# The attention stage's instructions put in an order computed by a list scheduler, with three PSUM tiles shared by mixing, scores and v's products

## The chip, the cores and the metric

The kernel runs on one core of a Trainium2 chip. The metric is the device time of one execution in microseconds, as the median of several runs; smaller is better. All five engines of the core work side by side, each through its own list of instructions in the order in which the program issues them: TensorE (PE; PEld are its weight loads), VectorE (DVE), ScalarE (ACT), GpSimd (POOL) and SyncE (SP). An instruction that waits holds up what stands behind it on its engine. POOL, SP and ACT also issue the transfers (DMA).

## The reference

Talking-heads attention, followed by a feed-forward part with a learned slope for negative values:

```python
scores = scale * np.matmul(q, k.transpose(0, 1, 3, 2))          # q, k, v: (4, 12, 448, 64)
scores = np.einsum('bhij,hg->bgij', scores, w_pre)              # heads are mixed
scores = scores - np.max(scores, axis=-1, keepdims=True)
attn = np.exp(scores)
attn = attn / (np.sum(attn, axis=-1, keepdims=True) + 1e-09)
attn = np.einsum('bhij,hg->bgij', attn, w_post)                 # and mixed again
x = np.matmul(attn, v)                                          # -> (1792, 768)
h = x @ w_in                                                    # w_in: (768, 2048), float64
g = np.maximum(h, 0.0) + alpha * np.minimum(h, 0.0)
out = g @ w_out                                                 # (1792, 768), w_out float64
```

## The kernel before

**Tiling.** Each of the 4 batches is cut into four chunks of query rows: 120, 120, 120 and 90 (`CHUNKS`, L27; two rows of the last chunk are computed twice). There are NC = 16 chunks. A chunk is cut again into groups of 10 rows with all 12 heads, 120 rows in all; there are NG = 180 groups, and two groups make one step, NB = 90 steps. A step is called m, and it has these parts:

- *Scores, Q* (`qk`, L143): six tiles for each chunk, 96 in all; a tile holds two heads, four matmuls of 64 x 64, or 64 x 56 in a chunk of 120 and 64 x 26 in a chunk of 90 for the second part of the rows. `qk_out` (L158) copies the tile from PSUM to an SBUF tile st, one of three (`NXS`).
- *Relay, L* (`relay`, L167): a transfer from SBUF to SBUF that gathers one group's rows and heads (210 KB) into one of eight buffers sr.
- *Mixing, M* (`mix`, L172): two groups times the mask matrix `wk`, into a PSUM tile m.
- *Maximum, R* (`rmax`, L181, DVE), *exponentials, E* (`exp`, L186, ACT, two of them), *normalising, N* (`norm`, L193, DVE, three small ones).
- *Products with w_post, P* (`post`, L204): 56 small matmuls into the PSUM tile pa, of which there is one; `post_out` (L218, called A below) copies pa in two parts to the chunk's tile at.
- *v's products, V* (`pv`, L227): two for each chunk, 48 matmuls of 128 x 64 each; `pv_out` (L239) makes an upper half (ACT, XH) and a lower half (DVE, XL) in the tile xe and leaves two stores to the scratch x2 in DRAM for the next step.

**PSUM.** It has eight banks. Mixing has two tiles of two banks (`ps_m`), scores and v's products share one tile of two banks (`ps_s`), pa has the last two (L102 to L104).

**Order.** The order is written by hand in `step(m)` (L371): the loads of this step, mixing of m + 1, the stores left over, relays up to three steps ahead, `norm(m - 1)`, `rmax(m + 1)`, `exp(m)`, one scores tile, `post(m - 2)` and its copies, then the rest of the scores and v's products. A table `jobs` (L283 to L304) says in which step the scores, the v products and the loads of q, k and v come; scores tiles come 0.92 steps apart (`WPACE`). Relays go out by SP and POOL in turn; q, k, v and raw weights are loaded by POOL, x2 and wsc are stored by SP. VectorE also turns the first three blocks of the two float64 weights into float32 (`convert`, L269, 42 operations spread over the steps), which go to the scratch wsc and are read back and split before the feed-forward part (`load_pre`, `split_w`).

**Feed-forward.** 64 units (`units`, L413) of 18 matmuls `l1`, four operations `act` and 18 matmuls `l2`. Units 0 and 1 of `l1` are issued inside the last attention steps (L553 to L558).

Of the kernel before, what the change touches and what calls it, by code (L numbers as in the profile page):

```python
# [14 lines left out]
ALU = mybir.AluOpType  # L15
# [26 lines left out]
WPACE = 0.92  # L42


def round_f64(nc, raw, e, t):
# [15 lines left out]
    yield lambda: v.tensor_tensor(tf, tf, e.bitcast(F32), ALU.mult)  # L61


@with_exitstack
def talking_heads_prelu(ctx: ExitStack, tc: tile.TileContext, q, k, v, w_pre, w_post, mask, w_in, w_out, alpha, out):
# [23 lines left out]
    p1, p1r, p1m = ExitStack(), ExitStack(), ExitStack()  # L89
# [22 lines left out]
    pa = ps_a.tile([128, 2, 512], F32, tag="a", name="pa")  # L112
# [30 lines left out]
    def qk(ci, p, ps_pool=None):  # L143
        b, c = chunk_list[ci]
        cn = CHUNKS[c][1]
        ps = (ps_pool or ps_s).tile([128, 2, 512], F32, tag="m" if ps_pool else "s", name=f"s{ci}_{p}")
# [11 lines left out]
    def qk_out(ci, p, copy=nc.scalar.copy):  # L158
        if p == 0:
            s_t[ci] = s_tile(ci % NXS, f"st{ci}")  # L160
# [6 lines left out]
    def relay(n, dma):  # L167
        ci, r = groups[n]
        sr_t[n] = sr_b[n % NSR]
        dma.dma_start(out=sr_t[n][SR0:SR0 + GP], in_=s_t[ci][r:CHUNKS[chunk_list[ci][1]][1]:CHUNKS[chunk_list[ci][1]][1] // GI])  # L170

    def mix(m):  # L172

        ps = ps_m.tile([128, 2, 512], F32, tag="m", name=f"m{m}")
# [43 lines left out]
    def post_out(m):  # L218
        for g in range(2):
            n = 2 * m + g  # L220
            ci, r = groups[n]
            if n == first[ci]:
                a_t[ci] = a_tile(f"at{ci}")[:, :NS * H * CW].rearrange("p (s h i) -> p s h i", s=NS, h=H)
            dst = a_t[ci].rearrange("p s h i -> p (s h) i")[:, :, GI * r:GI * r + GI]
            nc.vector.tensor_copy(dst, pa[:, g, :NS * GP].rearrange("p (s i) -> p s i", i=GI))  # L225

    def pv(ci, hx, ps_pool=None):  # L227
        b, c = chunk_list[ci]
        cn = CHUNKS[c][1]
        ps = (ps_pool or ps_s).tile([128, 2, 512], F32, tag="m" if ps_pool else "s", name=f"x{ci}_{hx}")  # L230
# [8 lines left out]
    def pv_out(ci, hx):  # L239
        b, c = chunk_list[ci]  # L240
        c0, cn = CHUNKS[c]
        xe = xep.tile([128, 2, 3, CW], F32R, tag="xe", name=f"xe{ci}_{hx}")
        ps = u_t.pop(("pv", ci, hx))
        hi, lo = (xe[:, i, :, :cn].rearrange("p c (k g) -> p c g k", k=GI) for i in range(2))
        src = ps[:, 0, :3 * CW].rearrange("p (c i) -> p c i", c=3)[:, :, :cn].rearrange("p c (g k) -> p c g k", k=GI)
        nc.scalar.copy(hi, src)  # L246
        nc.vector.tensor_tensor(lo, src, hi, ALU.subtract)  # L247

        def store():
            for i in range(2):  # L250
                nc.sync.dma_start(
                    out=x2[i, 3 * hx:3 * hx + 3, :, b * S + c0:b * S + c0 + cn].rearrange("c p i -> p c i"),
                    in_=xe[:, i, :, :cn].bitcast(F32))

        later.append(store)

    later = []
# [11 lines left out]
    def convert():  # L269
        todo = [(f, x) for f in range(NPRE) for x in range(2)]  # L270
        raw_c = [fetch_w(*todo[0])]
        yield
        for i, (f, x) in enumerate(todo):
            if i + 1 < len(todo):
                raw_c.append(fetch_w(*todo[i + 1]))
            t, ops = round_w(f, x, raw_c.pop(0))
            for op in ops:
                op()
                yield
            later.append(lambda f=f, x=x, t=t: nc.sync.dma_start(  # L280
                out=wsc[f, :, x * DM:(x + 1) * DM], in_=t.bitcast(F32)))

    jobs = {}  # L283

    def at(m, f, *args):
        jobs.setdefault(m, []).append((f, args))

    LEAD = 4
    uses = [(ci, p) for ci in range(1, NC) for p in range(NP)][LEAD:]
    for i, (ci, p) in enumerate(uses):  # L290
        at(int(i * WPACE), "qk", ci, p)
        b, c = chunk_list[ci]
        if c == len(CHUNKS) - 1 and b + 1 < B and p in (1, 3):
            at(int(i * WPACE) + 1, "load", load_k, b + 1, (p + 1) // 2)
    for ci, (b, c) in enumerate(chunk_list):
        if ci >= 2:
            at(max(first[ci - 2] // 2 - 1, 0), "load", load_q, ci)
        if c == 0:
            if b:
                at(first[ci] // 2 - 15, "load", load_k, b, 0)  # L300
            at(first[ci] // 2 + LAG + 3 if b else 1, "load", load_v, b)
        lb = (first[ci + 1] - 1) // 2
        at(lb + LAG + 1, "pv", ci, 0)
        at(lb + LAG + (2 if ci + 1 < NC else 1), "pv", ci, 1)  # L304
    conv_steps = NPRE * 2 * 7 + 1

    with tc.manual_schedule():
# [10 lines left out]
        def warm_up(n, name):  # L318
            ps = ps_m.tile([128, 2, 512], F32, tag="m", name=name)
# [21 lines left out]
        conv = convert()  # L341
        next(conv)
# [10 lines left out]
        relayed = 0  # L353

        def relays(upto, dmas):
            nonlocal relayed
            while relayed < min(upto, NG):
                relay(relayed, dmas[relayed % len(dmas)])
                relayed += 1

        for i in range(NP + LEAD):
            ci, p = divmod(i, NP)
            qk(ci, p, None if i % 3 == 2 else ps_m)
            qk_out(ci, p, nc.vector.tensor_copy if i % 2 else nc.scalar.copy)
            if i == NP - 1:
                relays(2 * (RAHEAD + 1), (nc.sync, nc.scalar, nc.gpsimd))
        done = 0
        live = lambda m: 0 <= m < NB
        EV = {"qk": (qk, qk_out), "pv": (pv, pv_out)}

        def step(m):  # L371
            nonlocal done
            todo = jobs.get(m, [])
            for f, args in todo:
                if f == "load":
                    args[0](*args[1:])
            uses = sorted([(f, args) for f, args in todo if f != "load"], key=lambda x: x[0] == "pv")
            early = 0 if not uses or uses[0][0] == "pv" else 1
            if live(m + 1):
                mix(m + 1)  # L380
            now, later[:] = list(later), []
            for f in now:
                f()
            if m >= 0:
                relays(2 * (m + 2 + RAHEAD) if m > 2 else first[1], (nc.sync, nc.gpsimd))
            if live(m - 1):
                norm(m - 1)
            if live(m + 1):
                rmax(m + 1)
            if live(m):  # L390
                exp(m, 0)
                exp(m, 1)
            for f, args in uses[:early]:
                EV[f][0](*args)
                EV[f][1](*args)
            if live(m - LAG):
                post(m - LAG)
                post_out(m - LAG)
            for f, args in uses[early:]:
                EV[f][0](*args)  # L400
                EV[f][1](*args)
            want = (m - 4) * conv_steps // (NB - 24)
            while done < want and done < conv_steps:
                next(conv, None)
                done += 1

# [10 lines left out]

        def load_x(bl, i):
# [5 lines left out]

        x_log, x_in = [], {}
# [17 lines left out]
        def split_w(f, x, src):  # L443
            t = (wi_t, wo_t)[x][f]
            nc.scalar.copy(t[:, 0], src)  # L445
            nc.vector.tensor_tensor(t[:, 1], src, t[:, 0], ALU.subtract)
# [27 lines left out]
        def l1(u):  # L474
            gi, bl, f = units[u]
            w, x = wi_t[f], x_t[bl].bitcast(F32R)
            ps = P2["h"].tile([128, 512], F32, tag="h", name=f"h{u}")
# [7 lines left out]

        def act(u):
            f = units[u][2]
            h = h_t.pop(u)[:, :S]
            t = P2["gp"].tile([128, S], F32, tag="t", name=f"t{u}")
            g = g_t[u] = P2["gp"].tile([128, 2, S], F32R, tag="g", name=f"g{u}")  # L490
            nc.scalar.activation(out=t, in_=h, func=AF.Relu, scale=-1.0)  # L491
            nc.vector.scalar_tensor_tensor(out=t, in0=t, scalar=oma[:, f:f + 1], in1=h, op0=ALU.mult, op1=ALU.add)  # L492
            nc.scalar.copy(g[:, 0], t)  # L493
            yield
            nc.vector.tensor_tensor(g[:, 1], t, g[:, 0], ALU.subtract)
            yield
# [150 lines left out]
```

## Time and profile before

| | us |
|---|---|
| runs shown | 996.95, 1007.74, 999.22 |
| median | 999.22 |
| the profiled execution's own time | 1001.84 |
| its span, first to last instruction | 1000.1 |

The profile is of one execution. Busy times over the whole span: PE 907.2 us (91%), its weight loads 669.0, DVE 596.1, ACT 319.9, POOL 110.6; the mean granted clock of TensorE is 0.957 of full speed, where 0.5 is its lower level (1.2 GHz) and 1.0 the upper (2.4 GHz). A PE that reads as busy need not be at its peak: matmuls are pipelined and their ends are modelled, so the time from the start of one group to the start of the next is the safer price. "Idle before, released by" names what ended an engine's wait.

### The profile page before, as it was taken

Reading aid. Unit: us, or ns where it says so; the run is one execution under the profiler, and the core shown is the slowest. Engines: PE = TensorE matmul, PEld = TensorE weight load, DVE = VectorE, ACT = ScalarE, POOL = GpSimd, SP = SyncE. Lnnn points to the kernel's source line nnn. Section 1 sums busy time; section 2 is a strip of 40 time slices with the busy share of each in tenths; the row PEclk is TensorE's granted clock in tenths of the full one; section 3 lists DMA queues with packets and bytes.
Section 4 is the critical chain, followed back from the end, with each engine's and each line's share of the span. In section 5 each row is a group of like instructions: output and inputs, shape, how many; then the busy total and the mean of one; then the engine's idle time right before and its main releaser. Section 6 shows DMA issues by size and latency. Waiting matters only on the chain.

```text
span 1000.1 us, 23702 instructions
## 1 busy us (share of the span) xinstructions
PE 907.2 (91%) x10380; PEld 669.0 (67%) x10380; DVE 596.1 (60%) x1085; ACT 319.9 (32%) x656; POOL 110.6 (11%) x193
## 2 busy tenths in 40 slices
PE   6899887998879988799589999999999999979998
PEld 2344553445534455245379999999999999869997
DVE  3556875468743787346565665766766765683222
ACT  2534553345532555233332222212112221221111
POOL 3312212111122120201000000000000000000000
PEclk9799998899978999798899999999999999989999
DMA  6764647446373464524966113201410330024111
GB/s 157 220 161 136 192 139 201 121 131 206 124 211 90 124 186 149 147 67 132 322 167 256 40 64 133 73 32 64 173 63 33 118 119 32 32 64 166 56 50 61
DMA packets 71022, 125.34 MB, mean 125 GB/s; under 512 B 32584, under 2 KB 59336, under 8 KB 70920
## 3 DMA queue, kind: packets, MB, share of 16 engines
q0 software_dynamic: 15264, 59.00, 19.6%
q1 hardware_dynamic: 54866, 63.33, 19.5%
q10 hardware_dynamic: 790, 1.52, 0.6%
q8 instruction: 81, 1.33, 0.6%
q14 instruction: 21, 0.17, 0.1%
HBM read 66.16 MB, written 18.92 MB: 85 GB/s over the span
## 4 chain that ended last, share of the span: by engine, by line
PE 74%; DVE 12%; DMA 7%; ACT 5%; issue 1%; POOL 1%; SPq 0%; DVEq 0%; ACTq 0%; POOLq 0%
PE h L481 23%; PE acc L508 22%; PE s L151 13%; PE x L235 8%; PE pa L212 5%; DMA sr<-st 3%; DMA q<-in_q_dram 3%; DVE at L225 3%; PE m L178 2%; ACT xe L246 2%; DVE xe L247 2%; DVE nm L183 2%; ACT st L163 2%; DVE ao L520 1%; DVE r L200 1%
## 5 line engine op out<-in xcount | busy, mean ns | idle before, releaser
L481 PE MATMUL h<-x,w 128*128 128x448 f32 x1152 | 251.2, 371 | 7.3 <-ACT w L445 6.9
L508 PE MATMUL acc<-g,w 128*128 128x448 f32 x1152 | 245.5, 366 | 2.1 <-DVE xe L247 1.5
L481 PEld LDWEIGHTS h<-x,w 128*128 128x128 f32 x1152 | 217.5, 189 | 30.2 <-ACT w L445 7.4
L508 PEld LDWEIGHTS acc<-g,w 128*128 128x128 f32 x1152 | 216.1, 188 | 21.5 <-DVE xe L247 1.6
L151 PE MATMUL s<-k,q 64*64 64x448 f32 (+2 forms) x768 | 174.6, 586 | 48.1 <-DMA q<-in_q_dram 18.2
L225 DVE COPY at<-pa 128x480 f32<-128x480 f32 x180 | 109.5, 649 | 101.8 <-PE pa L212 101.8
L212 PEld LDWEIGHTS pa<-r,e 64*64 64x64 f32 x5040 | 101.2, 142 | 74.0 <-DVE at L225 37.1
L151 PEld LDWEIGHTS s<-k,q 64*64 64x64 f32 (+2 forms) x768 | 40.1, 133 | 165.1 <-issue 102.7
L492 DVE SCALAR_TENSOR_TENSOR t<-t,oma,h 128x448 f32<-128x448 f32 x64 | 43.5, 679 | 154.8 <-ACT t L491 154.8
L163 ACT COPY st<-s 120x896 f32<-120x896 f32 (+1 forms) x91 | 82.2, 905 | 146.4 <-PE s L151 139.3
L190 ACT ACTIVATE e<-m,nm 128x448 f32<-128x448 f32 x180 | 112.2, 631 | 49.0 <-DVE nm L183 28.5
L212 PE MATMUL pa<-r,e 64*64 64x60 f32 x5040 | 109.4, 231 | 12.3 <-DVE at L225 11.0
L491 ACT ACTIVATE t<-h 128x448 f32<-128x448 f32 x64 | 34.8, 544 | 264.6 <-PE h L481 264.6
L178 PE MATMUL m<-sr,wk 64*64 64x448 f32 x720 | 98.5, 591 | 12.2 <-DMA sr<-st 12.0
L183 DVE TENSOR_REDUCE nm<-m 128x2 f32<-128x896 f32 x90 | 97.5, 1084 | 18.1 <-PE m L178 18.1
L235 PE MATMUL x<-at,v 128*64 128x120 f32 (+1 forms) x1536 | 81.9, 262 | 5.7 <-issue 2.1
L170 POOL DMA_DIRECT2D sr<-st x88 | 54.0, 614 | 276.4 <-PE m L178 200.8
L235 PEld LDWEIGHTS x<-at,v 128*64 128x64 f32 x1536 | 74.6, 137 | 9.7 <-ACT st L163 3.3
L247 DVE TENSOR_TENSOR xe<-x,xe 128x360 fp32r<-128x360 f32 (+1 forms) x32 | 24.0, 750 | 62.5 <-ACT xe L246 62.5
L520 DVE TENSOR_TENSOR ao<-ao,acc 128x448 f32<-128x448 f32 x96 | 52.6, 612 | 1.7 <-PE acc L508 1.7
L493 ACT CAST g<-t 128x448 fp32r<-128x448 f32 x64 | 36.3, 567 | 54.0 <-DVE t L492 54.0
L246 ACT CAST xe<-x 128x360 fp32r<-128x360 f32 (+1 forms) x32 | 24.2, 756 | 89.3 <-PE x L235 89.3
(47 smaller groups left out, 467.6 us busy)
## 6 DMA issues: line engine op xcount, KB each, us to landing
x<-x SPq DMA_DIRECT2D x16, 1344.0 KB
sr<-st SPq DMA_DIRECT2D x89, 210.0 KB
sr<-st POOLq DMA_DIRECT2D x88, 210.0 KB, 3.8
cr<-in_w_in_dram POOLq DMA_DIRECT2D x16, 768.0 KB, 4.7
cr<-in_w_out_dram POOLq DMA_DIRECT2D x16, 768.0 KB, 4.6
x<-xe SPq DMA_DIRECT2D x48, 180.0 KB
out_dram<-ao SPq DMA_DIRECT2D x24, 224.0 KB
v<-in_v_dram POOLq DMA_DIRECT2D x4, 1152.0 KB, 8.6
```

The lines of the kernel that those rows point to most:

```text
L151: nc.tensor.matmul(ps[i0:i1, hf, :S], q_t[ci][r, p * cn + i0:p * cn + i1], k_t[b, p // 2][r, p % 2, :], start=True, stop=True)
L163: copy(dst[:cn, p], u_t.pop(("qk", ci, p))[:cn, :, :S])
L170: dma.dma_start(out=sr_t[n][SR0:SR0 + GP], in_=s_t[ci][r:CHUNKS[chunk_list[ci][1]][1]:CHUNKS[chunk_list[ci][1]][1] // GI])
L178: nc.tensor.matmul(ps[hf:hf + 64, u, :S], wk[r, :], g[r, :], start=True, stop=True)
L183: nc.vector.tensor_reduce(out=nm, in_=m_t[m][:, :, :S], axis=AX.X, op=ALU.max, negate=True)
L190: nc.scalar.activation(out=e_t[m][:, u], in_=m_t[m][:, u, :S], func=AF.Exp, bias=nm_t[m][:, u:u + 1], scale=1.0, accum_out=se_t[m][:, u:u ...
L212: nc.tensor.matmul(dst[:, :, HI * u:HI * u + HI], e[h, u, 64 * jb:64 * jb + 64], r[h, u].rearrange("p (h i) -> p h i", h=H), start=True, s ...
L225: nc.vector.tensor_copy(dst, pa[:, g, :NS * GP].rearrange("p (s i) -> p s i", i=GI))
L235: nc.tensor.matmul(ps[64 * t:64 * t + 64, 0, cl * CW:cl * CW + cn], v_t[b][:, s, h * D:(h + 1) * D], a_t[ci][:, s, h, :cn], start=(s == 0) ...
L481: nc.tensor.matmul(ps[:, :S], w[:, tw, cc * 128:(cc + 1) * 128], x[:, tx, cc, :], start=(i == 0), stop=(i == 3 * NCC - 1))
L508: nc.tensor.matmul(accs[c][:, :S], w[:, tw, c * 128:(c + 1) * 128], g[:, tg], start=(f == fs[0] and i == 0), stop=(f == fs[-1] and i == 2))
L520: nc.vector.tensor_tensor(acc_sb[c, bl], acc_sb[c, bl], accs[c][:, :S], ALU.add)
```

## The change

`plan` is new. It lists every operation of the attention stage with the engines that may do it, a duration from `COST`, a priority counted in steps, the operations that it needs, and the buffers that it takes and gives back. A loop then picks, again and again, the operation with the smallest start time + 0.3 x priority, and the list sorted by start time is the order in which the program issues. Mixing, scores, v's products and the first two units of `l1` each take one of three PSUM tiles of two banks; pa stays alone. The copies S, A and XH go to ACT or DVE, as the planner finds. The waits between engines are made from the data, as before; the plan sets the order alone. `step`, `jobs`, `convert` and `later` go. The transfers are planned as one lane (dma), and each operation is issued by the same engine as before; relays alternate, the first six over SP, ACT and POOL. The feed-forward part's loop stays, but for units 0 and 1, whose `act` is planned too, and the PSUM pool of `h`, which opens later. The diff, cut:

```diff
-WPACE = 0.92
+COST = {"Q": 0.82, "M": 0.82, "P": 1.0, "V": 2.15, "U": 3.7, "mode": 0.15, "R": 1.09, "E": 1.37, "N": 0.68}
+HOP, DRAIN = 0.07, 0.2
+LOOK = 0.3
+def plan(groups, first, chunk_list):
+    for ci, (b, c) in enumerate(chunk_list):
+        op(("LQ", ci), dma(1.0) if ci >= 2 else dma(0.0, 0.0), first[max(ci - 1, 0)] / 2 - RAHEAD - 5, acq=(("q", ci),))
+        for p in range(NP):
+            n = ci * NP + p
+            prio = (n - NP) * 0.92 - 1
+            op(("Q", ci, p), pe("Q"), prio, [("LQ", ci), ("LK", b, p // 2)], (("slot", (ci, p)),) + ((("st", ci),) if p == 0 else ()),
+               ((("q", ci),) if p == NP - 1 else ()) + ((("k", b, p // 2),) if c == len(CHUNKS) - 1 and p % 2 else ()),
+               at=5.5 + 1.1 * p if ci == 0 else 10.0)
+            op(("S", ci, p), [act(0.92), dve(1.09)], prio, [("Q", ci, p)], rel=(("slot", (ci, p)),))
+    for b in range(B):
+        op(("LV", b), dma(3.0), f4 / 2 + (4 if b else 0), acq=(("v", b),), at=18.0)
+    for n, (ci, r) in enumerate(groups):
+        op(("L", n), dma(0.8, 4.0), n / 2 - 1 - RAHEAD, [("S", ci, p) for p in range(NP)], (("sr", n),),
+           (("st", ci),) if n + 1 == first[ci + 1] else ())
+    for m in range(NB):
+        op(("M", m), pe("M"), m - 1, [("L", 2 * m), ("L", 2 * m + 1)], (("slot", m),), (("sr", 2 * m), ("sr", 2 * m + 1)), at=12.0)
+        op(("R", m), dve(COST["R"]), m - 1, [("M", m)])
+        op(("E", m), act(COST["E"]), m, [("R", m)], (("e", m),), (("slot", m),))
+        op(("N", m), dve(COST["N"]), m + 1, [("E", m)], (("r", m),))
+        op(("P", m), pe("P"), m + 2, [("N", m)], (("pa", m),), (("e", m), ("r", m)))
+        for g in range(2):
+            op(("A", m, g), [act(0.52), dve(0.63)], m + 1.7, [("P", m)],
...
+            op(("V", ci, hx), pe("V", "v"), pr, mine + [("LV", b)], (("slot", (ci, hx, "v")),),
+            op(("XH", ci, hx), [act(0.8), dve(0.78)], pr, [("V", ci, hx)], (("xe", (ci, hx)),))
+            op(("XL", ci, hx), dve(0.78), pr, [("XH", ci, hx)], rel=(("slot", (ci, hx, "v")),))
+            op(("W", ci, hx), dma(1.0), pr + 1, [("XL", ci, hx)], rel=(("xe", (ci, hx)),))
...
+    cap = {"slot": 3, "st": NXS, "sr": 2 * (RAHEAD + 1), "e": LAG + 1, "r": LAG + 1, "pa": 1, "at": 2, "q": 3, "k": 4, "v": 1,
+           "xe": 2, "cr": 2, "ct": 2}
+    while ready:
+        best = None
+        for n in ready:
+            engs, prio, preds, acq, rel, at = ops[n]
+            if any(not free[kind] for kind, *_ in acq):
+                continue
+            t0 = max([at] + [end[p] for p in preds] + [min(free[kind])[0] for kind, *_ in acq])
+            for e, d, l, md in engs:
+                d += COST["mode"] if e == "PE" and md != mode else 0.0
+                t = max(t0, idle[e])
+                if best is None or (t + LOOK * prio, t) < best[0]:
+                    best = (t + LOOK * prio, t), n, e, d, l, md
...
+    return sorted(out)
@@
-    ps_m = pool("ps_m", 2, p1m, space=PSUM, side="right")
-    ps_s = pool("ps_s", 1, p1, space=PSUM)
-    ps_a = pool("ps_a", 1, p1, space=PSUM)
+    ps = pool("ps", 1, p1, space=PSUM)
+    pa = ps.tile([128, 2, 512], F32, tag="a", name="pa")
+    def slot_tile(i, name):
+        return ps.tile([128, 2, 512], F32, tag=f"b{i}", name=name)
@@
+    def relay_q(n, sr):
+        turns[0] += 1
+        dmas = (nc.sync, nc.scalar, nc.gpsimd) if n < 2 * RAHEAD else (nc.sync, nc.gpsimd)
+        relay(n, dmas[turns[0] % len(dmas)], sr)
@@
+        for _, _, n, e, got in plan(groups, first, chunk_list):
+            emit(n, e, got)
         p1.close()
         open_pool("ao", 1)
+        open_pool("h", 2, space=PSUM)
         open_pool("acc", 1, space=PSUM)
+        conv2 = convert2()
         next(conv2)
...
-            todo = [act(u)] if u < nu else []
+            todo = [act(u)] if 1 < u < nu else []
```

## Rows read from the trace of the kernel before

**Rows 1.** Stages: span, then busy of PE, PEld, DVE, ACT, POOL; clock, DMA share, GB/s.
```profile
25.70:520.50 494.80, 422.96 (x8020) 234.95 (x8020) 304.69 (x624) 218.46 (x487) 88.21 (x149) 0.92 0.54 161
...
164.00:186.00 22.00, 17.36 (x150) 5.47 (x150) 8.31 (x19) 5.17 (x13) 3.99 (x7) 0.77 0.77 209
...
284.00:312.00 28.00, 22.19 (x152) 6.65 (x152) 8.36 (x19) 5.19 (x13) 2.93 (x5) 0.63 0.51 141
...
406.00:422.00 16.00, 10.94 (x75) 3.42 (x76) 3.04 (x7) 2.24 (x5) 0.19 (x1) 0.57 0.53 155
422.00:484.00 62.00, 53.77 (x1054) 29.61 (x1052) 37.76 (x82) 24.21 (x61) 6.11 (x11) 0.94 0.42 135
...
520.50:1000.10 479.60, 468.59 (x2268) 427.04 (x2268) 281.24 (x442) 95.71 (x163) 12.91 (x24) 0.99 0.25 87
```

**Rows 2.** Order of time, PE, a step of wide scores: start, us, instruction.
```profile
237.67 0.98 PE L151 MATMUL s<-k,q 64*56 64x448 f32 x8
...
238.66 1.09 PE L212 MATMUL pa<-r,e 64*64 64x60 f32 x54
...
240.34 0.98 PE L151 MATMUL s<-k,q 64*56 64x448 f32 x8
```

**Rows 3.** Order of time, PE, a step with v's products.
```profile
230.85 2.68 PE L235 MATMUL x<-at,v 128*64 128x120 f32 x48
...
233.46 0.98 PE L178 MATMUL m<-sr,wk 64*64 64x448 f32 x8
...
235.24 0.98 PE L151 MATMUL s<-k,q 64*64 64x448 f32 x8 [0.80 <-DVE xe L247]
...
236.04 1.04 PE L212 MATMUL pa<-r,e 64*64 64x60 f32 x54
```

**Rows 4.** Order of time, PE and its weight loads, chunks of 90 rows.
```profile
53.69 3.52 PE L151 MATMUL s<-k,q 64*64 64x448 f32 x8
...
54.52 0.12 PEld L151 LDWEIGHTS s<-k,q 64*26 64x26 f32 x2 [0.71 <-issue]
...
57.14 1.09 PE L212 MATMUL pa<-r,e 64*64 64x60 f32 x54
...
513.48 2.08 PE L235 MATMUL x<-at,v 128*64 128x90 f32 x48
```

**Rows 5.** Waits of PE, 25.7 to 520.5: us in all, times, longest.
```profile
PE s L151 <- DMA q<-in_q_dram: 18.2, 3, 6.7
PE s L151 <- DVE xe L247: 18.2, 25, 0.8
PE m L178 <- DMA sr<-st: 12.0, 4, 7.6
PE pa L212 <- DVE at L225: 11.0, 17, 1.5
```

**Rows 6.** Order of time, POOL and PE, around the late load of q.
```profile
156.82 0.73 POOL L137 MEMSET v<- 64x768 f32 x1 [8.58 <-PE x L235]
...
158.84 1.06 POOL L131 DMA_DIRECT2D q<-in_q_dram  x2
...
168.64 6.64 PE L151 MATMUL s<-k,q 64*64 64x448 f32 x8 [5.04 <-DMA q<-in_q_dram]
```

**Rows 7.** Groups by shape, DVE and ACT, 25.7 to 520.5: count, busy, mean ns, idle.
```profile
L225 DVE COPY at<-pa 128x480 f32<-128x480 f32 x180 | 109.5, 649 | 101.8 <-PE pa L212 101.8
L183 DVE TENSOR_REDUCE nm<-m 128x2 f32<-128x896 f32 x90 | 97.5, 1084 | 18.1 <-PE m L178 18.1
...
L163 DVE COPY st<-s 120x896 f32<-120x896 f32 x1 | 1.1, 1091 | 4.4 <-PE s L151 4.4
...
L190 ACT ACTIVATE e<-m,nm 128x448 f32<-128x448 f32 x180 | 112.2, 631 | 49.0 <-DVE nm L183 28.5 <-PE pa L212 19.5 <-PE m L178 0.8
L163 ACT COPY st<-s 120x896 f32<-120x896 f32 x62 | 56.2, 906 | 27.2 <-PE s L151 25.8 <-DMA sr<-st 1.1
```

**Rows 8.** Transfers issued 156 to 176: count, KB each, median us to landing.
```profile
sr<-st POOLq DMA_DIRECT2D x4, 210.0 KB, 10.1
```

More of the change, by code (lines that the diff above doesn't have):

```diff
@@ L216, in a_tile, with post_out, pv @@
         return ap_.tile([128, 2 * 4 * DM], F32, tag="a", name=name)
[L218 to L227, printed above, removed]
+    def post_out(m, g, eng):
+        n = 2 * m + g
+        ci, r = groups[n]
+        if n == first[ci]:
+            a_t[ci] = a_tile(f"at{ci}")[:, :NS * H * CW].rearrange("p (s h i) -> p s h i", s=NS, h=H)
+        dst = a_t[ci].rearrange("p s h i -> p (s h) i")[:, :, GI * r:GI * r + GI]
+        copy_on[eng](dst, pa[:, g, :NS * GP].rearrange("p (s i) -> p s i", i=GI))
+    def pv(ci, hx, slot):
         b, c = chunk_list[ci]
         cn = CHUNKS[c][1]
-        ps = (ps_pool or ps_s).tile([128, 2, 512], F32, tag="m" if ps_pool else "s", name=f"x{ci}_{hx}")
+        ps = slot_tile(slot, f"x{ci}_{hx}")
         for cl in range(3):
@@ L237, in pv, with pv_out, store_x @@
         u_t["pv", ci, hx] = ps
-    def pv_out(ci, hx):
+    xe_t = {}
+    def pv_out(ci, hx, part, eng):
+        cn = CHUNKS[chunk_list[ci][1]][1]
+        if part == 0:
+            xe_t[ci, hx] = xep.tile([128, 2, 3, CW], F32R, tag="xe", name=f"xe{ci}_{hx}")
+        xe, ps = xe_t[ci, hx], u_t["pv", ci, hx]
+        hi, lo = (xe[:, i, :, :cn].rearrange("p c (k g) -> p c g k", k=GI) for i in range(2))
+        src = ps[:, 0, :3 * CW].rearrange("p (c i) -> p c i", c=3)[:, :, :cn].rearrange("p c (g k) -> p c g k", k=GI)
+        if part == 0:
+            copy_on[eng](hi, src)
+        else:
+            nc.vector.tensor_tensor(lo, src, hi, ALU.subtract)
+    def store_x(ci, hx):
         b, c = chunk_list[ci]
         c0, cn = CHUNKS[c]
[L242 to L257, printed above, removed]
+        for i in range(2):
+            nc.sync.dma_start(
+                out=x2[i, 3 * hx:3 * hx + 3, :, b * S + c0:b * S + c0 + cn].rearrange("c p i -> p c i"),
+                in_=xe_t[ci, hx][:, i, :, :cn].bitcast(F32))
     def fetch_w(f, x, dma=nc.gpsimd):
@@ L267, in round_w, with fetch, conv_op, store_w @@
         return t, round_f64(nc, raw, e, t)
[L269 to L305, printed above, removed]
+    half = lambda i: divmod(i, 2)
+    conv = {}
+    def fetch(i):
+        conv[i] = [fetch_w(*half(i))]
+    def conv_op(i, j):
+        if j == 0:
+            t, ops = round_w(*half(i), conv[i][0])
+            conv[i] = [t, list(ops)]
+        conv[i][1][j]()
+    def store_w(i):
+        f, x = half(i)
+        nc.sync.dma_start(out=wsc[f, :, x * DM:(x + 1) * DM], in_=conv[i][0].bitcast(F32))
     with tc.manual_schedule():
@@ L318, in warm_up @@
         def warm_up(n, name):
-            ps = ps_m.tile([128, 2, 512], F32, tag="m", name=name)
+            ps = slot_tile(2, name)
             for _ in range(n):
@@ L352, in talking_heads_prelu @@
         )
[L353 to L405, printed above, removed]
         P2 = {}
@@ L472, in convert2, with l1 @@
                 yield NFC
-        def l1(u):
+        def l1(u, slot=None):
             gi, bl, f = units[u]
             w, x = wi_t[f], x_t[bl].bitcast(F32R)
-            ps = P2["h"].tile([128, 512], F32, tag="h", name=f"h{u}")
+            ps = P2["h"].tile([128, 512], F32, tag="h", name=f"h{u}") if slot is None else slot_tile(slot, f"h{u}")[:, 0]
             i = 0
@@ L484, in l1, with act_op @@
             h_t[u] = ps
-        def act(u):
[L487 to L495, printed above, removed]
+        def act_op(u, j):
+            f = units[u][2]
+            h = h_t[u][:, :S]
+            if j == 0:
+                g_t[u] = (P2["gp"].tile([128, S], F32, tag="t", name=f"t{u}"),
+                          P2["gp"].tile([128, 2, S], F32R, tag="g", name=f"g{u}"))
+            t, g = g_t[u]
+            if j == 0:
+                nc.scalar.activation(out=t, in_=h, func=AF.Relu, scale=-1.0)
+            elif j == 1:
+                nc.vector.scalar_tensor_tensor(out=t, in0=t, scalar=oma[:, f:f + 1], in1=h, op0=ALU.mult, op1=ALU.add)
+            elif j == 2:
+                nc.scalar.copy(g[:, 0], t)
+            else:
+                nc.vector.tensor_tensor(g[:, 1], t, g[:, 0], ALU.subtract)
+        def act(u):
+            for j in range(4):
+                if j == 3:
+                    yield
+                act_op(u, j)
             yield
@@ L526, in talking_heads_prelu @@
         l2_done = 0
-        last = max(jobs)
-        end1 = max(NB + LAG, last + 1)
-        split_at = None
-        for m in range(-1, end1 + 1):
-            step(m)
-            if m == first[NC - 1] // 2 - RAHEAD + 1:
-                load_x(0, (NC - 3) % NXS)
-            if relayed == NG and split_at is None:
-                p1r.close()
-                open_pool("gp", 2, side="right")
-                open_pool("wA", 1, side="right")
-                for f in range(2):
-                    load_pre(f)
-                load_x(1, (NC - 2) % NXS)
-                conv2 = convert2()
-                split_at = m + 4
-            elif split_at is not None and 0 <= m - split_at < NPRE:
-                f = m - split_at
-                w_tile(f)
-                for x in range(2):
-                    split_w(f, x, wr[f][:, x * DM:(x + 1) * DM])
-                if f + 2 < NPRE:
-                    load_pre(f + 2)
-            if m == NB - 1:
-                p1m.close()
-                open_pool("h", 2, space=PSUM, side="right")
-            if m == NB:
-                l1(0)
-            if m == NB + 1:
-                for _ in act(0):
-                    pass
-                l1(1)
@@ L559, in talking_heads_prelu, with split_pre, turn @@
-        for f in later:
-            f()
+        def split_pre(f, x, part):
+            if x == 0 and part == 0:
+                w_tile(f)
+            split_w(f, x, wr[f][:, x * DM:(x + 1) * DM], part)
+        def turn():
+            p1r.close()
+            open_pool("gp", 2, side="right")
+            open_pool("wA", 1, side="right")
+        turns = [0]
+        def relay_q(n, sr):
+            turns[0] += 1
+            dmas = (nc.sync, nc.scalar, nc.gpsimd) if n < 2 * RAHEAD else (nc.sync, nc.gpsimd)
+            relay(n, dmas[turns[0] % len(dmas)], sr)
```

142 lines of the change are left out of this document (124 added, 18 removed).

## The prediction

> **What bounds the kernel now.** I read the busy table by stage first [rows 1], because the change touches one stage only. Attention fills the span up to 520.5 us, where the feed-forward part starts its steady run; from there TensorE is busy 468.59 of 479.60 us at a granted clock of 0.99. No edit reaches into that run, so I carry its 479.6 us over unchanged. From the first mixing product at 25.7 us to 520.5, 494.8 us, the mean clock is 0.92; VectorE is busy 304.69 us and ScalarE 218.46 us. The two together are 523 us, 262 each if shared evenly: neither need be the bound. PE reads 422.96 us there, but busy PE is modelled and holds waits, so I price its work from the time between starts.
>
> The order of time gives these prices at full clock. The products P (L212) and the mixing M (L178) together take 1.68 us, 238.66 to 240.34, where the next scores start, and a whole step from scores to scores 2.67, 237.67 to 240.34 [rows 2]. A scores tile Q (L151) takes 0.80, 235.24 to 236.04; a tile V of v's products (L235) 2.61, 230.85 to 233.46 [rows 3]. The surprise is the scores of the chunks with 90 rows: 53.69 to 57.14, 3.45 us for the same count of matmuls, with weight loads of 26 columns 0.71 us apart, so its parts run one after another [rows 4]. There are 24 of those (4 batches, 6 each). V of such a chunk takes about 2.0 (2.08 busy, [rows 4]).
>
> PE's work from 25.7 us on: 90 x 1.68 = 151 for P and M; some 62 wide scores tiles x 0.80 = 50 (72 in all, some ten run before); 24 x 3.45 = 83; 24 x 2.61 + 8 x 2.0 = 79; two first-layer units of the feed-forward part, which run before 520.5 already, 7 (18 matmuls each, at 468.59 us for the 2268 records left, [rows 1]). Together 370 us, against 494.8. So 125 us of attention are waits and low clock, and that is what there is to win.
>
> The waits of PE tell where they lie [rows 5]. Three waits for a load of q are 18.2 us; 25 waits for the lower half of v's products (xe, L247) 18.2; 17 waits for the copies of P's output 11.0; four waits for relayed rows 12.0. The waits on xe are longer than the table says: M starts at 233.46 and needs 0.80, Q starts at 235.24, so PE stood 0.98 [rows 3]; 25 of these are 25 us. The waits for q bring more with them. POOL's queue shows the cause [rows 6]: the load of the next v waits 8.58 us for v's last products, and a load of q stands behind it, issued at 158.84, landed only at 168.64. PE then runs the scores at half clock, 6.64 us in place of 3.45. In the three windows around these stalls the clock is 0.77, 0.63 and 0.57 [rows 1], which is 22 x 0.46 + 28 x 0.74 + 16 x 0.86 = 45 us at 1.2 GHz; less about 8 of them idle, half of the rest is lost, 18 us. So the late q costs 18 + 18 = 36 us.
>
> **The change, part by part.**
>
> *Shared PSUM tiles.* Before, scores and v's products shared one tile, and mixing had two. A scores tile behind V waited for V, its ScalarE copy and the VectorE subtraction. With three shared tiles the 25 us should nearly go; I leave 3. The new price is that mixing may wait for a tile. A tile is held by M some 3.7 us (M 0.98, maximum 1.08, two exponentials of 0.63 [rows 3, 7] and their hand-overs), by Q 2.05 (4.6 for 90 rows), by V 4.4: 90 x 3.7 + 62 x 2.05 + 24 x 4.6 + 32 x 4.4 = 711 us over three tiles, 237 each, below PE's 370. So tiles aren't the bound, but PE takes its instructions in order, and a mixing product that waits holds everything behind it; that is in the allowance below.
>
> *Copies on either engine.* Copies of P's output (180, 0.649 us on VectorE), of scores and the upper half of v's products may go to ScalarE. ScalarE doing the P copies isn't in the trace; the nearest row is the scores copy, 0.906 on ScalarE against 1.091 on VectorE [rows 7], which gives 0.54; no gain per copy would be 0.65. I take 0.54 to 0.65; either end leaves both engines near 262 us. The 11 us of waits for these copies can shrink, but a tighter schedule makes new ones.
>
> *Order of the loads.* Each load of q is planned as soon as one of three q buffers is free, without standing behind v. A load of q for the 90-row chunk then goes out some steps before v's. The 36 us should mostly go. What stays is the crowd at the three batch borders: relayed rows took 10.1 us to land near 160 [rows 8], while the planner books 4.0. Relays run three steps ahead, about 10 us, so I leave 10 us for the borders.
>
> *Relays, stores, first weight fetches.* Relays keep alternating SP and POOL; stores are no longer put off by one step; the first weight fetch moves out of the start. All that is hidden behind PE; if the cover went (SP stuck on a relay whose buffer PE has not freed), x's stores and the loads behind them come late, and the nearest price is the 7.6 us in which the last mixing products waited for their relay, part of the 12.0 [rows 5]. I leave 10 us for it at the end, and 8 for the start, where mixing waits for relays under either order (the other 4.4 us of the 12.0, and by my estimate as much in slow clock beside them).
>
> *The planner's book.* It charges 0.82 us for every scores tile; the 90-row ones take 3.45. So 24 x 2.63 = 63 us are not in the plan. PE doesn't lose them twice: while it is late, VectorE and ScalarE catch up. The parts of the trace with only wide tiles are another matter: there PE needs 2.48 us a step, and the planner must keep VectorE and ScalarE near 3 us a step of PE's 3.4 (with V). I charge 10% of PE's work without the 90-row tiles and the steps that go with them, some 225 us: 22 us. Bounds: 0 to 20% of the whole 370, 74 us. I take the 22 because the step of [rows 2] takes 2.67 for 2.48 of work, about nine tenths, with the old order.
>
> The Trainium skill (TensorEngine Tiling (Array Packing), section Key Properties) says that a change of the tiling mode drains TensorE; the 0.71 us steps between 64- and 26-column loads [rows 4] agree. By that rule the cost hangs on the shape and no order wins it back; were it the order's doing, 24 x 2.65 = 64 us more would go and the time would be near 880.
>
> *Sum.* 25.7 + 370 + 22 + 3 + 10 + 10 + 8, and 7 for low clock in the phases of 90-row scores that no late load explains, is 456 in place of 520.5. That saves 65; some waits have no name in my list, and I keep 10 for them: 55. The profiled execution took 1001.84 us, so about 947; the median of the runs, 999.22, is 2.6 lower, so **944 us**.
>
> **The rivals.**
>
> *The forecast, chance 0.65:* 920 to 966.
>
> *The plan holds nearly perfectly, 0.07:* all named losses but the start go, 25.7 + 370 + 8 + 10 = 414, time near 895, up to 920.
>
> *The plan breaks around the mispriced scores, 0.18:* PE arrives 2.63 us late at each of 24 tiles, and an order made for another time leaves the chain maximum, exponentials, normalising (1.08 + 2 x 0.63 + an estimated 0.6 = 2.9 us) bare behind half of them: 35 us of 55 go back, 979. For it: the same engines carry copies that were planned as if both were free at a certain time. Against it: a late PE lets the other engines get ahead. It reaches up to no change, so 0.12 of it is faster by over 1%, and 0.06 within 1%.
>
> *TensorE's clock falls through all phases of 90-row scores, slower, 0.10:* these phases run the narrowest products. At 1.2 GHz such a tile takes 6.64 [rows 6], 3.2 more, and what goes with it (P, M and a share of V, 2.6 us) doubles: 5.8 us a tile. A few of the 24 run so already, as that one, behind a long idle. Ten more at half clock eat the 55 us, twelve make the kernel slower by 1%, and twenty cost 116 and give 1060. For it: the clock is only 0.94 between 422 and 484 us [rows 1], where no load was late. Against it: the new order has fewer idle stretches ahead of them. The Trainium skill (TensorE: Matmul & The Clock Gate, section What's actually happening) makes half rate the resting state, which the engine's own activity releases; by that a fuller PE would lose even the 7 us I left, and the time would be 937.
>
> **How the numbers follow.** A measurement of this kernel can tell about 1% from no change. Faster: 0.65 + 0.07 + 0.12 = 0.84; within 1%: 0.06; slower: 0.10. The range goes from 905, inside the perfect plan, to 995, where the 74 us bound in place of 22 puts the sum (944 + 52 = 996) and the broken plan ends; outside lie the slower case, part of the no-change case and half of the perfect plan, less than 0.2.
>
> **What would show it.** Right: no wait of PE for q, waits for xe under 3 us, the copies of P's output split over VectorE and ScalarE, steps with a V near 5.1 us (2.48 + 2.61), the steady run of the feed-forward part starting near 465 us and as long as before. Wrong: the 90-row tiles no longer at 3.45 us; a granted clock below 0.9 over those phases; PE waiting for mixing's tile or for relays by tens of us; a feed-forward run other than 479.6 us.

## The result and the profile after

| | before | after |
|---|---|---|
| median, us | 998.09 | 935.49 |
| ratio, 95% interval | | 0.9392 [0.9324, 0.9461] |
| span of the profiled execution | 1000.1 | 934.0 |
| mean granted clock | 0.957 | 0.985 |
| feed-forward run starts at | 520.5 | 455.06 |

Some executions run longer at a lower clock; the ratios here and below leave them out, so they differ a little from the quotient of the medians. 944 was forecast, 905 to 995; the change gives 6.1%, and the medians are 62.6 us apart. All of it lies ahead of the feed-forward run. The busy times by stage for the kernel after (span, then PE, PEld, DVE, ACT, POOL, clock, DMA share, GB/s), to be held against [rows 1]:

```profile
21.52:455.06 433.54, 393.12 (x7996) 230.41 (x7996) 287.68 (x562) 238.42 (x546) 84.76 (x144) 0.98 0.64 183
455.06:934.00 478.94, 468.29 (x2268) 426.78 (x2268) 280.62 (x441) 95.83 (x163) 12.71 (x24) 0.99 0.25 87
```

The second line is the run that no edit reaches: 478.94 us against 479.60. The first is attention from the first mixing product on: 433.5 us in place of 494.8, at a clock of 0.98 in place of 0.92, with 17 us less on VectorE and 20 more on ScalarE. Of these 61 us, 31 are time in which PE was idle (494.80 - 422.96 = 71.8 before, 433.54 - 393.12 = 40.4 after), and 30 are time in which it was busy with the same work; the low clock of before lies in the latter. The first mixing product comes at 21.52 instead of 25.7.

The waits of PE in the kernel after, against [rows 5] (us in all, times, longest):

```profile
PE m L313 <- DMA sr<-st: 18.4, 11, 6.8
PE pa L347 <- issue: 9.4, 6, 3.0
...
PE pa L347 <- DVE at L359: 4.5, 5, 1.4
PE m L313 <- ACT e L325: 1.9, 4, 0.5
...
PE s L286 <- DVE xe L385: 0.3, 1, 0.3
```

The wait of scores for q, 18.2 us before, is gone from the list; the one for xe fell from 18.2 to 0.3, the one for the copies of P's output from 11.0 to 4.5. The wait for relayed rows grew from 12.0 to 18.4: it is now the largest. By the order of time 11.9 us of it lie ahead of 48 us, and the other 6.5 within 20 us behind the loads of v for the second and third batch; the longest of either kind:

```profile
32.87 1.01 PE L313 MATMUL m<-sr,wk 64*64 64x448 f32 x2 [6.76 <-DMA sr<-st]
...
264.60 0.59 PE L313 MATMUL m<-sr,wk 64*64 64x448 f32 x2 [2.91 <-DMA sr<-st]
```

The 9.4 us of "issue" are six waits for which the profile shows no cause; three of them, 6.3 us, lie at 256, 364 and 372 us, also behind a load of v. A step with v's products in order of time, PE and the VectorE instruction that gives the tile free, against [rows 3]:

```profile
204.72 2.68 PE L369 MATMUL x<-at,v 128*64 128x120 f32 x48
...
207.33 0.98 PE L313 MATMUL m<-sr,wk 64*64 64x448 f32 x8
...
208.13 1.10 PE L347 MATMUL pa<-r,e 64*64 64x60 f32 x56
...
208.28 0.81 DVE L385 TENSOR_TENSOR xe<-x,xe 128x360 fp32r<-128x360 f32 x1 [0.55 <-ACT xe L383]
...
209.14 0.98 PE L286 MATMUL s<-k,q 64*64 64x448 f32 x8
```

Scores come at 209.14, and PE has stood nowhere in between: mixing and P fill the time in which xe is made. Behind it, the copies of P's output in the kernel after, by engine (count, busy, mean ns, idle before):

```profile
L359 DVE COPY at<-pa 128x480 f32<-128x480 f32 x83 | 53.8, 656 | 54.8 <-ACT at L359 30.4 <-PE pa L347 24.2
L359 ACT COPY at<-pa 128x480 f32<-128x480 f32 x97 | 53.8, 570 | 69.7 <-PE pa L347 55.1 <-DVE at L359 14.4
```

97 of the 180 went to ScalarE, at 0.570 us. The step with v's products takes 5.22 us up to the end of its scores (204.72 to 209.94, where they take 0.80), near the 5.1 of the forecast.

### The profile page after: what moved, and what is told of

Read it like the earlier page. It is cut to its first block, busy times and chain, and to the rows that moved or that the text cites. A ratio compares the mean times of both kernels' runs of the same rounds, so it can differ in the third digit from the quotient of the medians.

```text
span 934.0 us, 23852 instructions
## 1 busy us (share of the span) xinstructions
PE 878.8 (94%) x10380; PEld 665.5 (71%) x10380; DVE 578.4 (62%) x1023; ACT 343.5 (37%) x718; POOL 110.6 (12%) x194
## 4 chain that ended last, share of the span: by engine, by line
PE 82%; DVE 6%; DMA 6%; ACT 3%; issue 2%; SPq 0%; POOL 0%; ACTq 0%; DVEq 0%; POOLq 0%
PE h L541 25%; PE acc L579 24%; PE s L286 13%; PE x L369 8%; PE pa L347 7%; PE m L313 7%; DMA sr<-st 5%; DVE at L359 1%; DVE nm L318 1%; ACT e L325 1%; DVE ao L591 1%; ACT st L299 1%; ACT at L359 1%; DMA k<-in_k_dram 1%; DVE ct L60 0%
## 5 line engine op out<-in xcount | busy, mean ns | idle before, releaser
L286 PE MATMUL s<-k,q 64*64 64x448 f32 (+2 forms) x768 | 159.9, 555 | 1.9 <-ACT st L299 0.6
L347 PE MATMUL pa<-r,e 64*64 64x60 f32 x5040 | 105.8, 223 | 14.6 <-issue 9.4
L313 PE MATMUL m<-sr,wk 64*64 64x448 f32 x720 | 97.7, 566 | 21.6 <-DMA sr<-st 18.4
L286 PEld LDWEIGHTS s<-k,q 64*64 64x64 f32 (+2 forms) x768 | 37.2, 128 | 78.2 <-issue 65.0
L359 DVE COPY at<-pa 128x480 f32<-128x480 f32 x83 | 53.8, 656 | 54.8 <-ACT at L359 30.4
L299 ACT COPY st<-s 120x896 f32<-120x896 f32 (+1 forms) x65 | 58.6, 906 | 67.7 <-PE s L286 61.2
L359 ACT COPY at<-pa 128x480 f32<-128x480 f32 x97 | 53.8, 570 | 69.7 <-PE pa L347 55.1
L313 PEld LDWEIGHTS m<-sr,wk 64*64 64x64 f32 (+1 forms) x720 | 24.9, 134 | 55.1 <-DMA sr<-st 22.2
```

Source lines behind the costliest of these rows:

```text
L313: nc.tensor.matmul(ps[hf:hf + 64, u, :S], wk[r, :], g[r, :], start=True, stop=True)
L347: nc.tensor.matmul(dst[:, :, HI * u:HI * u + HI], e[h, u, 64 * jb:64 * jb + 64], r[h, u].rearrange("p (h i) -> p h i", h=H), start=True, s ...
L359: copy_on[eng](dst, pa[:, g, :NS * GP].rearrange("p (s i) -> p s i", i=GI))
```

## The experiments

My theory (A): the late load of q cost 36 us, the tile shared by scores and v's products 25, the copies some 5 to 10, and each part of the change takes its own share away. Rivals: the gain is the even share of copies (B); single parts give less, because a stall that is removed comes back as another (C); the planned order does it without shared tiles (D). Ratios are to the kernel before, with 95% intervals.

| kernel | ratio | interval |
|---|---|---|
| before, q's load ahead of v's (b_q) | 0.9834 | 0.9746 to 0.9922 |
| before, three PSUM tiles in turn (b_ps) | 0.9957 | 0.9900 to 1.0013 |
| before, both (b_q_ps) | 0.9816 | 0.9758 to 0.9874 |
| before, 90-row scores up to three steps later (b_late) | 1.0058 | 1.0009 to 1.0107 |
| before, wider second part of 90-row scores (b_pad) | 0.9346 | 0.9262 to 0.9430 |
| after, copies bound to their old engines (a_nosplit) | 0.9459 | 0.9401 to 0.9518 |
| after, PSUM tiles parted 2 + 1 (a_sep) | 0.9736 | 0.9688 to 0.9784 |
| after, parted and bound (a_sep_nosplit) | 0.9656 | 0.9582 to 0.9730 |
| after, q's load behind v's (a_lateq) | 0.9369 | 0.9319 to 0.9419 |
| after, right price of 90-row scores (a_cost90) | 0.9415 | 0.9359 to 0.9472 |
| after, second part 56 columns wide (a_pad) | 0.8900 | 0.8869 to 0.8932 |
| after, second part 34 columns wide (a_pad34) | 0.8802 | 0.8718 to 0.8886 |

### Parts alone, in the order by hand

b_q sorts a step's loads:

```diff
-            for f, args in todo:
-                if f == "load":
-                    args[0](*args[1:])
+            loads = [args for f, args in todo if f == "load"]
+            for args in sorted(loads, key=lambda x: x[0] is not load_q):
+                args[0](*args[1:])
```

> The kernel before with one part alone: within a step the load of q is issued ahead of v's. Theory A (the late load of q cost 36 us, and the loads' order wins it): 998 - 36 = about 962 us, no wait of PE for q, clock near 1.0 in the three batch borders. Rival B (the gain is the even share of the copies between VectorE and ScalarE, the loads count for little): 985 to 998. Rival C (only the whole order helps; the stall taken away comes back as another wait, a relay's or v's): waits of 10 us or more for relays at the borders, 975 to 990.

b_ps takes all tiles from one pool of three (the first two units of `l1` as well), b_q_ps has both edits:

```diff
-    ps_m = pool("ps_m", 2, p1m, space=PSUM, side="right")
-    ps_s = pool("ps_s", 1, p1, space=PSUM)
+    ps_m = pool("ps_m", 3, p1, space=PSUM)
...
-        ps = (ps_pool or ps_s).tile([128, 2, 512], F32, tag="m" if ps_pool else "s", name=f"x{ci}_{hx}")
+        ps = ps_m.tile([128, 2, 512], F32, tag="m", name=f"x{ci}_{hx}")
```

> The kernel before with another part alone: three PSUM tiles taken in turn by mixing, scores and v's products, the order by hand otherwise kept. Theory A (25 us of waits behind v's products go): about 973 us, the wait of scores for xe under 3 us. Rival B: 990 to 998. Rival C (in the old order a tile taken in turn makes mixing wait for exponentials or scores for mixing's tile): PE waits for ACT e instead, 985 to 1005.

> Both parts together in the order by hand. Theory A: they add up, 998 - 61 = about 937 us, within 10 us of the changed kernel's 935, which leaves the planner's order and its shared copies next to nothing. Rival B: 960 or more. Rival C: 955 to 975, because the old order keeps VectorE full in the steps without v's products.

Measured: b_q wins some 17 us (1.7%) in place of 36, b_ps nothing that can be told from no change, both together 18 in place of 61. Theory A falls; rivals B and C both come within a few us of these times, and only a_nosplit below parts them. The waits of PE in b_q_ps show what is left:

```profile
PE s L150 <- DVE xe L246: 19.0, 26, 0.8
PE m L177 <- DMA sr<-st: 17.0, 5, 7.5
PE pa L211 <- DVE at L224: 12.4, 19, 1.8
```

No wait for q is left. A little of it comes back as a wait for relayed rows, 4.23 us at the first border (the 17.0 hold 7.46 at the end of the stage, where the kernel before has 7.58). The wait for xe is as long as with one shared tile. The order of time shows one:

```profile
129.94 0.98 PE L177 MATMUL m<-sr,wk 64*64 64x448 f32 x8
...
130.88 0.78 DVE L246 TENSOR_TENSOR xe<-x,xe 128x360 fp32r<-128x360 f32 x1 [2.22 <-ACT xe L245]
...
131.72 0.98 PE L150 MATMUL s<-k,q 64*64 64x448 f32 x8 [0.80 <-DVE xe L246]
```

The order by hand issues mixing of m + 1 before the exponentials of m, so mixing holds two of the three tiles at that point, and the next scores get the tile of v's products, as before. In this order the third tile does not help; the planned one puts other work in between.

### The 90-row scores later

```diff
-        at(int(i * WPACE), "qk", ci, p)
+        at(int(i * WPACE) + ((3, 2, 2, 1, 1, 0)[p] if ci > 3 and chunk_list[ci][1] == 3 else 0), "qk", ci, p)
```

> The kernel before with the six scores tiles of the last three batches' 90-row chunks issued up to three steps later (by 3, 2, 2, 1, 1, 0 steps), the loads untouched. Theory E (the planned order got rid of the stall by asking for these scores three steps later, not by the earlier load): no wait of PE for q, clock above 0.9 at the borders, 965 to 985 us. Theory F (the crowd of transfers at the border costs the time, whoever waits for it): the wait moves to relays or to v, 988 to 1000 us.

The planned order asks for the first 90-row scores of the second batch after 34 mixing products, the one by hand after 31. b_late copies that. It gains nothing, and its waits of PE tell that the stall has moved (us in all, times, longest; then the longest one in order of time):

```profile
PE m L178 <- DMA sr<-st: 33.4, 6, 9.9
...
181.56 1.77 PE L178 MATMUL m<-sr,wk 64*64 64x448 f32 x8 [9.89 <-DMA sr<-st]
```

No scores wait for q any more, but mixing now stands 9.89 us for its relay at the same border. That is the wait that theory F of that run foretold; that the crowd of transfers is its cause is argued from the rows. POOL's queue in b_late, where nothing of the loads was changed, and the landing times of what it issued between 160 and 184 us (KB each, median us):

```profile
162.94 0.73 POOL L137 MEMSET v<- 64x768 f32 x1 [8.58 <-PE x L235]
163.62 0.80 POOL L138 DMA_DIRECT2D v<-in_v_dram  x1
164.41 0.56 POOL L139 DMA_DIRECT2D v<-in_v_dram  x1
164.95 1.06 POOL L131 DMA_DIRECT2D q<-in_q_dram  x2
165.97 1.25 POOL L170 DMA_DIRECT2D sr<-st  x2
167.19 0.61 POOL L261 DMA_DIRECT2D cr<-in_w_out_dram  x1
167.76 0.64 POOL L170 DMA_DIRECT2D sr<-st  x1
...
sr<-st POOLq DMA_DIRECT2D x4, 210.0 KB, 10.9
cr<-in_w_out_dram POOLq DMA_DIRECT2D x1, 768.0 KB, 14.9
```

POOL stands 8.58 us for v's last products, and relays, q, and a weight block queue up behind and go out together within 5 us. The relays, issued late, then land in 10.9 us.

### The planned order with one part undone

a_nosplit binds the copies:

```diff
-            op(("S", ci, p), [act(0.92), dve(1.09)], prio, [("Q", ci, p)], rel=(("slot", (ci, p)),))
+            op(("S", ci, p), [act(0.92)] if ci else [act(0.92), dve(1.09)], prio, [("Q", ci, p)], rel=(("slot", (ci, p)),))
-            op(("A", m, g), [act(0.52), dve(0.63)], m + 1.7, [("P", m)],
+            op(("A", m, g), [dve(0.63)], m + 1.7, [("P", m)],
-            op(("XH", ci, hx), [act(0.8), dve(0.78)], pr, [("V", ci, hx)], (("xe", (ci, hx)),))
+            op(("XH", ci, hx), [act(0.8)], pr, [("V", ci, hx)], (("xe", (ci, hx)),))
```

> The changed kernel with the copies bound to the engines of before (P's output on VectorE, scores after the first chunk and the upper half of v's products on ScalarE), planned anew. Theory A (copies count for 5 to 10 us): 940 to 945 us. Rival B (the even share is the gain): 960 or more, VectorE busy over 95% in the steps without v's products and PE waiting for the copies of P's output by 20 us or more.

a_sep parts the tiles again (scores, v's products and the units U take "one", mixing two of "slot"):

```diff
-            op(("Q", ci, p), pe("Q"), prio, [("LQ", ci), ("LK", b, p // 2)], (("slot", (ci, p)),) + ((("st", ci),) if p == 0 else ()),
+            op(("Q", ci, p), pe("Q"), prio, [("LQ", ci), ("LK", b, p // 2)], (("one", (ci, p)),) + ((("st", ci),) if p == 0 else ()),
...
-    cap = {"slot": 3, "st": NXS, "sr": 2 * (RAHEAD + 1), "e": LAG + 1, "r": LAG + 1, "pa": 1, "at": 2, "q": 3, "k": 4, "v": 1,
+    cap = {"slot": 2, "one": 1, "st": NXS, "sr": 2 * (RAHEAD + 1), "e": LAG + 1, "r": LAG + 1, "pa": 1, "at": 2, "q": 3, "k": 4, "v": 1,
```

> The changed kernel, planned anew with the three PSUM tiles parted as before the change: two for mixing, one for scores, v's products and the first units of the feed-forward part. Theory A (a planned order needs the sharing to get rid of the 25 us behind v's products): 955 to 965 us, PE waits for xe or its copies by 15 us or more. Rival D (the order alone does it: the planner puts mixing, P and other work behind v's products until the tile is free): 935 to 943 us.

> The changed kernel planned anew with neither shared tiles nor copies on either engine: what is left of the change is the planned order. If the parts add up (sharing 29, copies 4): 965 to 972 us, so that the order alone is worth some 28 us of the 63. If sharing and the free choice of engine only work together: 975 us or more.

Parting the tiles costs 0.9736 - 0.9392 = 3.4%, 34 us, with copies free, and 2.0%, 20 us, with copies bound (a_nosplit against a_sep_nosplit); the medians give 29 and 24. A part of it belongs to the start: the kernel before let the first ten scores tiles use mixing's tiles too, these two runs do not, and their first mixing product comes 3.6 and 7.1 us later than in their counterparts. From there to the feed-forward run the profiled spans differ by 21 and 17 us. That is theory A's size, and rival D falls. Binding the copies costs 0.7% with shared tiles, and the two intervals overlap; with parted tiles the free choice brings nothing. Rival B falls. What is left with neither, the planned order alone, is 0.9656: 34 us. a_sep's waits of PE, over its whole span:

```profile
PE s L286 <- ACT st L299: 10.8, 15, 1.0
PE m L313 <- DMA sr<-st: 10.7, 5, 3.9
...
PE s L286 <- DVE xe L385: 4.2, 6, 1.2
```

The planner puts work behind v's products here too, so the wait for xe is 4.2 and not 18.2. Of the 10.8 in which scores wait for the copy of the last ones, 8.2 lie at the start and 2.6 behind the first mixing product. So the waits do not tell where the 21 us lie: in that stretch PE's idle time is only 6 us longer than in the kernel after (454.36 - 408.28 = 46.1 against 40.4), its busy time 15, and a busy PE can hold waits.

### The late load and the wrong price, in the planned order

a_lateq makes the load of q for 90-row chunks wait, in the plan, for the last v products of the batch before:

```diff
+        late = [("V", ci - 4, 1)] if b and c == len(CHUNKS) - 1 else []
-        op(("LQ", ci), dma(1.0) if ci >= 2 else dma(0.0, 0.0), first[max(ci - 1, 0)] / 2 - RAHEAD - 5, acq=(("q", ci),))
+        op(("LQ", ci), dma(1.0) if ci >= 2 else dma(0.0, 0.0), first[max(ci - 1, 0)] / 2 - RAHEAD - (0 if late else 5), late, acq=(("q", ci),))
```

> The changed kernel, planned anew with one dependence more: the load of q for a chunk of 90 rows waits in the plan for the last v products of the batch before, so that it stands behind v's load on POOL as before the change (three batch borders). Theory A (the late q is the larger part of the gain): 960 to 970 us, PE waits for q by 15 us, clock below 0.8 at the borders. Rival E (the new order asks for these scores three steps later, so a late q costs little): 935 to 945 us.

a_cost90 gives those scores a price of their own:

```diff
-COST = {"Q": 0.82,
+COST = {"Q": 0.82, "Q90": 3.45,
-            op(("Q", ci, p), pe("Q"), prio,
+            op(("Q", ci, p), pe("Q" if CHUNKS[c][1] == CW else "Q90"), prio,
```

> The changed kernel with the right price in the planner's book: 3.45 us in place of 0.82 for the 24 scores tiles of 90-row chunks. If the mispriced tiles broke the plan (rival of the prediction): 910 to 925 us. Theory A (a late PE lets the other engines catch up, the wrong price costs little): 928 to 940 us, within 1%.

Neither moves the time by what can be told. a_lateq is the miss that matters for my theory: q's load stands behind v's again, 13 us later, and no scores wait for it. POOL's queue and landing times there:

```profile
140.09 1.24 POOL L307 DMA_DIRECT2D sr<-st  x2 [9.54 <-ACT at L360]
142.26 0.73 POOL L270 MEMSET v<- 64x768 f32 x1 [0.93 <-PE x L370]
142.94 0.79 POOL L271 DMA_DIRECT2D v<-in_v_dram  x1
...
155.63 1.09 POOL L264 DMA_DIRECT2D q<-in_q_dram  x2
...
sr<-st POOLq DMA_DIRECT2D x7, 210.0 KB, 4.4
```

The load of v waits 0.93 us, against 8.58. POOL stands here too, 9.54 us, but at a relay; v follows in 2 us, and neither q nor a weight block goes out right behind it. Relays land in 4.4 us. That is not so at every border: in the kernel after, where POOL issued the second load of v, four relays and q over 8 us, the relays that it issued between 248 and 268 us took twice as long, and PE waited 2.91 us for one:

```profile
sr<-st POOLq DMA_DIRECT2D x5, 210.0 KB, 9.1
```

### The scores of 90 rows

The second part of these tiles (rows 64 to 89) gets more columns, the next head's or zeros, and the rows that come of them are never read; a_pad and b_pad make it 56 columns, a_pad34 34:

```diff
-                i0, i1 = 64 * ch, min(64 * ch + 64, cn)
+                i0, i1 = 64 * ch, min(64 * ch + 64, CW)
...
+        if cn < CW:
+            nc.gpsimd.memset(q_t[ci][:, NP * cn:NP * cn + CW - cn], 0.0)
```

> The changed kernel with the scores of a 90-row chunk computed as 64 and 56 columns in place of 64 and 26: the 30 columns more are the next head's or zeros (a small memset on POOL), and their rows are never read. If the 3.45 us hang on the shape of the second part: a tile takes 0.80 as the wide ones do, 24 x 2.65 = 64 us less PE work, and with VectorE and ScalarE near 3 us a step as the next bound 870 to 890 us. If they hang on anything else of these chunks: 930 to 940 us.

> The kernel before, order by hand and loads as they were, with the second part of a 90-row chunk's scores computed as 56 columns in place of 26 (the added columns are the next head's or zeros, their rows are never read). If PE's work is what the hand order waits for in those phases: 998 - 64 = about 934 us, as much as the whole planned order brings. If the hand order is held there by VectorE and by the waits behind v's products: 950 to 975 us.

> The changed kernel with the second part of a 90-row chunk's scores 34 columns wide, between the 26 of before (3.45 us a tile) and the 56 (0.80 us). If what counts is whether a part is wider than 32 columns, so that all four products have one tiling mode: 0.8 us a tile, 880 to 888 us. If the price goes with the width: between 895 and 925 us.

In the order by hand this alone wins 6.5%, 65 us, the 24 x 2.65 = 64 that were worked out, and as much as the whole planned order. In the planned order it wins 49 us with 56 columns and 59 with 34 (the two intervals touch). So a_pad34, median 877.38 us, beats both kernels by 12.0% and 6.3%. Its 0.75 us a tile fit the condition "wider than 32 columns" and not a price that goes with the width. Its order of time shows the price:

```profile
159.66 1.01 PE L315 MATMUL m<-sr,wk 64*64 64x448 f32 x8
160.41 1.01 PE L288 MATMUL s<-k,q 64*34 64x448 f32 x8
161.16 1.01 PE L315 MATMUL m<-sr,wk 64*64 64x448 f32 x8
```

0.75 us from start to start, in place of 3.45 [rows 4].

## Why the prediction was right, and where not

**What bounds it.** The untouched feed-forward run held, and no run contradicts PE's 370 us of work. The kernel after spends 433.5 us on that work from its first mixing product on, so about 63 of 125 us of waits and low clock are left. b_pad confirms the dearest term, 83 us for 24 tiles, by its saving. My reading of its rows was loose: 0.71 us is the idle time before the narrow weight loads, not their distance. The weight loads of the four parts start 0.83 to 0.90 us apart, and the four make the 3.45.

**Sum.** The feed-forward run was to start at 465, the unnamed 10 included, and started at 455.06. Of these 10 us, 4 are the earlier first mixing product. The others are the balance of the allowances, which came out one by one as follows: the wait for xe took 0.3 of 3; at the end no mixing product waited for its relay, where 10 were kept; the borders took 6.5 for relays and some 6 without a shown cause, of 10; the start overran, 11.9 us of waits for relays against 8. A mean clock of 0.98 over 433 us loses some 9 us at most, where 7 were kept. The sum came near because terms missed both ways, not because each was right.

**Shared tiles.** Right in size (22 us forecast; 20 and 34 measured in the planned order, 17 and 21 of it behind the first mixing product), wrong as a part of its own. That the waits for xe are where it lies is not shown: with the tiles parted, they are 4.2 us. "With three shared tiles the 25 us should nearly go" fails in the order by hand (b_ps): there the third tile is held by mixing. The tiles and the order make this gain together.

**Copies.** The price on ScalarE, 0.570 us, lies in the 0.54 to 0.65 given. Their worth, 0.7%, is not clear of nothing.

**Order of the loads: the step that failed.** I put 36 us on the late q, and its cure on q's load going out ahead of v's. The waits did go: none for q is left, of 18.2 us, and the clock rose to 0.98. But a_lateq has q behind v and loses nothing; b_q has q ahead of v and wins half; b_late frees the scores from q and mixing waits 9.89 us instead. q was only the first to be late. What the rows show in its place is a POOL queue that stood 8.58 us at a load put too early, and then sent everything at once; with q moved ahead it still stood 7.17 us there, and mixing then waited 4.23 us for a relay (b_q_ps). That the planned order wins by what it sends behind v is argued from those rows: its queue stands as long, at a relay, and its relays are not fast at every border (9.1 us at the second). No run changed v's load alone, or the weight block that goes out behind it in the order by hand, so how much of the order's 34 us lies there stays open.

**The planner's book.** Right: 63 us missing from the plan cost nothing that can be measured (a_cost90). My 22 us for the plan's own slack were not tested.

**The rivals.** The broken plan falls with a_cost90. The clock's fall over the 90-row scores did not come: the first pair and the last tile of the kernel after stand at full clock,

```profile
66.63 7.04 PE L286 MATMUL s<-k,q 64*64 64x448 f32 x16
...
401.96 3.52 PE L286 MATMUL s<-k,q 64*64 64x448 f32 x8
```

two tiles in 7.04 us and one in 3.52, and so do those between them. The Trainium skill (TensorE: Matmul & The Clock Gate, section What's actually happening), by which the engine's own activity releases the half rate, agrees here: with the idle stretches of 5.0 to 6.7 us before scores gone the attention clock went from 0.92 to 0.98, and from 32 to 36 us, behind the one wait as long that is left, 6.76 us, it was 0.50.

**The tiling rule.** I used the Trainium skill (TensorEngine Tiling (Array Packing), section Key Properties: a change of the tiling mode drains TensorE) to say that no order wins back the 90-row price. The order did not: 3.5 us after as before. That 34 columns cost 0.75 and 26 cost 3.45 agrees with the page's list of modes (section Available Configurations), in which a tile is 128, 64 or 32 columns wide; no run shows the mode itself.

## What to carry to other kernels

A wait in a trace names who came late, not why: before costing its removal, look at what else stands in the same queue and would be late next; here one cure of a wait gave half its price, another gave nothing, and undoing the cure in the planned order lost nothing. The same three buffers gave nothing in one order and some 20 us in another, so test them together with the order. And price from start to start: the mean busy times of the products with 64, 56 and 26 columns read 585, 573 and 633 ns, nearly alike, and hid 64 us, which a few unread columns win back.

## What the runs showed of the hardware

A set of four products on 64 x 64 tiles takes 0.75 to 0.80 us; with the second part of the columns 26 wide instead of 34 or 56, it takes 3.45, with an idle time of 0.71 us before its narrow weight loads [rows 4]. Relays of 210 KB landed in 10.9 us where v, q, a weight block and three relays went out within 5 us (b_late), and where POOL's issues were spread over 8 us in 4.4 (a_lateq, first border) or 9.1 (the kernel after, second border).
